# An attention and expert kernel: the router's early work in smaller steps, a pinned first phase, and products of zeros before the first tokens

## The chip, the cores and the metric

The kernel runs on one core of a Trainium2 chip. A core has a matrix engine (TensorE, PE in the profile, with its weight loads PEld), VectorE (DVE), ScalarE (ACT), GpSimd (POOL) and SyncE (SP), which issues transfers. Each engine takes its own list of instructions in order and waits on semaphores for the others. The metric is the time of one execution in microseconds (us), as the median of several runs; lower is better.

## The reference

```python
# attention: batch 8, heads 8, sequence 576, head size 64
scores = q @ k.T / 8 + slope[h] * -(i - j)      # kept where 0 <= i - j < 128
attn = softmax(scores); out = attn @ v
x = out.transpose(0, 2, 1, 3).reshape(4608, 512)
# experts: 8, each takes exactly 576 tokens
logits = x @ w_gate                              # 4608 x 8
# all 36864 (token, expert) pairs are gone through from the largest logit down;
# a token goes to the expert if it has none yet and the expert has room
for e in range(8):
    out[assigned == e] = relu(x[assigned == e] @ w1[e]) @ w2[e]   # 512 -> 1024 -> 512
```

## The kernel before

**Attention** goes over 32 pairs of heads (8 batches of 4 pairs). One iteration of its loop works on several pairs at once, in stages: `scores` and `least` of pair n (products of q and k on TensorE; then, on VectorE at L133, the bias and the row's least value), `exps` on ScalarE, `turn` and `turned` (u transposed on TensorE at L157, and copied to the tiles PT at L165, two of the four copies on VectorE), `av`, then `natural`, and `divide` (L240 to L255 on VectorE) of a pair four iterations older. Instructions put through `keep_in_program_order` stay in the order in which they are written; in attention that holds for TensorE, VectorE and ScalarE. The banks of PSUM that the transposes go to are four, and come free when the PT copies have been made.

**The router** needs, for each token, the best expert `am` and its logit `b` (`first_choice`: five operations b, ne, cand, am, OH). Logits `L_sb` have 36 columns of 128 tokens, four or five a batch; `logits` adds them up on GpSimd (L296 to L299) after a batch's last pair. Phase 0 finds the first expert that fills, by counting tokens over 64 thresholds in three rounds (`ends` for the range, `place`, `counts`, `enough`, `narrow`), then the list `idx` of its 576 tokens. Phases 1 to 7 do so for the others, in between the experts' products.

Some of phase 0 is done early. `early_counts` is a generator, made when the first 27 columns are there (batch 5), and `early_step` takes a step of it once a pair, directly behind `divide`. Its first step is `first_choice` over all 27 columns; then the range; then the indicators `ind` over 26 columns in two cuts, counted by 13 products of TensorE. In attention the router's instructions are pinned in written order through `OrderedCore`, so they show up in the trace under its line, L442, and `self.nc` is set back to the plain core before phase 0 itself, which is left to the scheduler.

**The experts** (`layer_moe`). `gather` issues five indirect transfers on GpSimd for an expert's tokens, `turn` transposes them (L832) and splits them into high and low parts (xh on ScalarE, xl on VectorE); weights come by SyncE as 512 KB chunks, and `split` makes their two parts. `layer1` (L853) and `layer2` (L878 to L881) are products in three terms. `slot` is called between pieces of these and hands out the router's steps, loads, splits and gathers. `layer2` goes over five pieces of tokens, t = 0 to 4; each result is stored by an indirect transfer of GpSimd (L891). Piece 4 has 64 tokens, and takes a copy and an addition on VectorE (L889, L890).

Of the kernel before, what the change touches and what calls it, by code (L numbers as in the profile page):

```python
# [25 lines left out]
def attention(tc, pools, qk_in, v_in, rel_in, C, x_dram, L_sb, router):  # L26
# [289 lines left out]
    for n in range(NPAIRS + LAG + 2):  # L316
# [92 lines left out]
WARM = 11  # L409
# [13 lines left out]
J = 64  # L423
CUTS = 2
STEPS = 3
FIRST = 27
EXACT_STEPS = 12
# [22 lines left out]
class Router:  # L450
# [5 lines left out]
    def __init__(self, tc, pools, C, L_sb):  # L456
# [3 lines left out]
        self.room, self.steps = None, iter(())  # L460
# [19 lines left out]
    def first_choice(self, L, b, am, OH, c0, c1):  # L480
# [8 lines left out]
        nc.vector.scalar_tensor_tensor(cand[:, :, 0:n], ne[:, :, 0:n], 16.0, eb, ALU.mult, ALU.add)  # L489
        nc.vector.tensor_reduce(am, cand[:, :, 0:n].rearrange("p e c -> p c e"), AX.X, ALU.min)  # L490
        nc.vector.tensor_tensor(OH, eb, bc(am.unsqueeze(1), [128, 8, n]), ALU.is_equal)

    def ends(self, b, top):
# [21 lines left out]
        if top:  # L515
# [6 lines left out]
            nc.vector.tensor_tensor(self.hi, ev[:, 1:2], sp, ALU.add)  # L522
        w = self.small("w")
# [23 lines left out]

    def counts(self, key, OH, th=None, c0=0, c1=NT):
# [6 lines left out]
        for a, z in zip(cuts, cuts[1:]):  # L555
            if th is None:
                nc.vector.tensor_tensor(ind[:, a:z, :].rearrange("p c (s o) -> p c s o", o=2),  # L557
                                        bc(key[:, a:z].unsqueeze(2), [128, z - a, J // 2, 2]),
                                        bc(self.C["i64"].rearrange("p (s o) -> p s o", o=2).unsqueeze(1), [128, z - a, J // 2, 2]),
                                        ALU.is_ge)  # L560
# [3 lines left out]
        yield WAITS[2]  # L564
        cnt = self.bank()
        for c in range(c0, c1, 2):
            nc.tensor.matmul(cnt[:, 0:16], ind[:, c:c + 2, :].rearrange("p c j -> p (c j)"),  # L567
                             OH[:, :, c:c + 2].rearrange("p e c -> p c e"), start=(c == c0), stop=(c == c1 - 2))
# [30 lines left out]

    def early_counts(self):  # L600
        nc = self.nc
        self.first_choice(self.L0, self.b0, self.am0, self.OH0, 0, FIRST)
        yield
        self.first = yield from self.ends(self.b0[:, 0:FIRST], True)
        lo, w, rw = self.first
        self.clamp(self.c0, self.b0, lo, w, 0, FIRST - 1)
        cnt = yield from self.counts(self.place(self.c0, lo, rw, 0, FIRST - 1), self.OH0, None, 0, FIRST - 1)
# [16 lines left out]
    def phase(self, k, exact=False):  # L624
# [6 lines left out]
        else:  # L631
            L, b, OH = self.L1, self.small("b", NT), rt.tile([128, 8, NT], BF, name="OH")
            am = rt.tile([128, NT], BF, name="am")
            self.first_choice(L, b, am, OH, 0, NT)
# [5 lines left out]
        else:  # L640
# [19 lines left out]
            nc.vector.scalar_tensor_tensor(self.hi, w, n[:, 0:1], low, ALU.mult, ALU.add)  # L660

        T1 = rt.tile([128, 8, NT], BF, name="T1")
        nc.vector.tensor_tensor(T1, OH, bc(sel.unsqueeze(1), [128, 8, NT]), ALU.mult)
        yield WAITS[4]
# [5 lines left out]
        keyv, mx, ef = self.small("keyv", 8), self.small("kmx"), self.small("ef")  # L670
        nc.vector.scalar_tensor_tensor(keyv, Dc, float(CAP), self.left, ALU.is_ge, ALU.mult)
        nc.vector.tensor_reduce(mx, keyv, AX.X, ALU.max)
        nc.vector.tensor_scalar(ef, mx, -1.0, 8.0, ALU.mult, ALU.add)

        m = rt.tile([128, NT], BF, name="m")
        nc.vector.scalar_tensor_tensor(m, am, ef[:, 0:1], sel, ALU.is_equal, ALU.mult)
# [4 lines left out]
        ei = rt.tile([128, 1], I32, name="ei", bufs=4)  # L681
        nc.vector.tensor_scalar(ei, ef, 7.0, None, ALU.min)
        self.ei[k] = ei
# [3 lines left out]
        nc.tensor.matmul(sp[:, 0:NT], self.C["tri"], m, start=False, stop=True)  # L687
        hi = self.small("hif", NT)
# [12 lines left out]
        if k == 0:  # L701
            nc.gpsimd.tensor_tensor(mv[:, :, 0, :], hOH, self.C["cc"], ALU.mult)
            nc.scalar.mul(mv[:, :, 1, :], hOH, self.C["pcol"][:, 0:1])
# [384 lines left out]
```

## Time and profile before

| | |
|---|---|
| median of 3 runs | 732.72 us (732.15 to 734.02) |
| the profiled execution | 731.64 us, its span 729.9 us |
| TensorE busy | 676.3 us (93%) |
| VectorE, ScalarE, GpSimd busy | 462.7, 330.8, 154.3 us |
| mean granted clock of TensorE | 0.964 |
| attention, to the last logits | 0 to 228 us |
| phase 0, to the first list of tokens | 228 to 247 us |
| first layer's first product to the last product | 258 to 716 us |

In the rows that follow, a timeline's row gives start, duration, engine, line, operation, output and inputs, shapes and count, and in brackets the engine's idle time ahead of it and what ended that. A window's row gives its length, then busy time and number of instructions for PE, PEld, DVE, ACT and POOL, then the granted clock (1.00 is full speed), the share of the transfer engines and GB/s.

### The profile page before, as it was taken

The numbers are of one execution on the slowest core, as the hardware profiler recorded it, in microseconds if no ns is written. First come the engines' busy times: TensorE is split into PE (matmuls) and PEld (weight loads), VectorE is DVE, ScalarE is ACT, GpSimd is POOL, SyncE is SP. The second block draws the span as 40 slices with busy tenths as digits, with TensorE's granted clock in tenths as the row PEclk, the third lists the DMA queues.
The fourth block names the chain that finished last, engine by engine and source line by source line (L and its number), as shares of the span: only waits on it lengthen the run. The fifth ranks groups of instructions, "written<-read, shape, count | busy, mean of one in ns | idle before, by whom it ended". The sixth has DMA issues, their size and how long they took to land.

```text
span 729.9 us, 19089 instructions
## 1 busy us (share of the span) xinstructions
PE 676.3 (93%) x7399; PEld 596.7 (82%) x7399; DVE 462.7 (63%) x1826; ACT 330.8 (45%) x990; POOL 154.3 (21%) x341
## 2 busy tenths in 40 slices
PE   7999999997976199999999999999999999999992
PEld 4998998996865188789889989989988988989981
DVE  6877777777775779869678828847856525413200
ACT  6988888887753252424232224324324324313100
POOL 4121222122120401423042131132123022011011
PEclk9999999999987589999999999999999999999996
DMA  8465655656312531617135235135135325101010
GB/s 298 137 219 165 211 187 167 203 169 201 97 54 67 194 103 58 253 52 242 69 118 200 84 106 173 59 116 159 59 118 170 102 92 184 60 30 37 1 44 26
DMA packets 35139, 92.73 MB, mean 127 GB/s; under 512 B 3808, under 2 KB 13152, under 8 KB 35040
## 3 DMA queue, kind: packets, MB, share of 16 engines
q1 hardware_dynamic: 29152, 72.55, 29.9%
q0 software_dynamic: 5888, 18.88, 8.0%
q8 instruction: 60, 0.98, 0.6%
q14 instruction: 39, 0.32, 0.2%
HBM read 72.54 MB, written 18.87 MB: 125 GB/s over the span
## 4 chain that ended last, share of the span: by engine, by line
PE 84%; DVE 8%; issue 2%; DMA 2%; POOL 1%; ACT 0%; POOLq 0%; SPq 0%; DVEq 0%
PE ph L853 27%; PE po L878 10%; PE po L879 10%; PE po L881 8%; PE s L53 7%; PE pt L53 6%; PE pt L157 6%; PE x L53 5%; DVE u L133 3%; PE pg L832 2%; PE m L567 2%; DMA g<-x,idx 2%; DMA rel_sb<-in_rel_dram 1%; DVE ind L557 1%; PE m L714 0%
## 5 line engine op out<-in xcount | busy, mean ns | idle before, releaser
L853 PE MATMUL ph<-xh,hl 128*128 128x288 f32 (+2 forms) x1024 | 192.6, 300 | 0.0
L853 PEld LDWEIGHTS ph<-xh,hl 128*128 128x128 f32 x1024 | 155.2, 189 | 0.9
L144 ACT ACTIVATE u<-u,mn 128x192 f32<-128x192 f32 (+2 forms) x288 | 123.8, 433 | 30.0 <-DVE mn L133 30.0
L878 PE MATMUL po<-hl,hh 128*128 128x512 f32 x320 | 129.3, 404 | 0.0
L879 PE MATMUL po<-hl,hh 128*128 128x512 f32 x320 | 125.0, 390 | 0.0
L853 PE MATMUL ph<-xl,hl 128*128 128x288 f32 (+2 forms) x512 | 116.1, 297 | 0.0
L859 ACT ACTIVATE hh<-ph 128x288 fp32r<-128x288 f32 (+2 forms) x128 | 46.6, 409 | 152.3 <-PE ph L853 143.6
L133 DVE CUSTOM_DVE_ANT_0 u<-s,bm 128x192 f32<-128x192 f32 x308 | 86.4, 333 | 41.6 <-PE s L53 41.1
L881 PE MATMUL po<-hl,hlo 128*128 128x512 f32 x256 | 100.4, 392 | 0.0
L806 DVE TENSOR_TENSOR hl<-raw,hl 128x512 fp32r<-128x512 f32 x128 | 84.8, 684 | 14.0 <-ACT hl L804 13.5
L891 POOL DMA_INDIRECT out_dram<-o,idx x40 | 44.1, 1102 | 205.6 <-ACT o L886 145.8
L853 PEld LDWEIGHTS ph<-xl,hl 128*128 128x128 f32 x512 | 84.2, 189 | 0.1
L834 DVE TENSOR_TENSOR xl<-pg,xh 128x512 fp32r<-128x512 f32 (+1 forms) x37 | 23.6, 639 | 86.6 <-ACT xh L833 86.6
L864 DVE SCALAR_TENSOR_TENSOR hlo<-ph,hh 128x288 fp32r<-128x288 f32 (+2 forms) x128 | 49.5, 417 | 40.8 <-ACT hh L859 40.3
L804 ACT CAST hl<-raw 128x1024 fp32r<-128x1024 f32 x64 | 65.4, 1048 | 17.1 <-DMA raw<-in_w_dram 9.3
L53 PE MATMUL s<-qk 64*64 64x192 f32 (+1 forms) x1112 | 70.5, 326 | 2.2 <-DVE mn L133 2.1
L878 PEld LDWEIGHTS po<-hl,hh 128*128 128x128 f32 x320 | 60.2, 188 | 11.5
L879 PEld LDWEIGHTS po<-hl,hh 128*128 128x128 f32 x320 | 60.2, 188 | 11.1
L157 PE MATMUL pt<-ident_sb,u 128*128 128x128 f32 x368 | 54.5, 283 | 9.8 <-DVE PT L165 8.3
L886 ACT COPY o<-po 128x512 f32<-128x512 f32 x32 | 18.8, 587 | 89.6 <-PE po L881 59.1
L881 PEld LDWEIGHTS po<-hl,hlo 128*128 128x128 f32 x256 | 48.0, 188 | 10.7
L815 POOL DMA_INDIRECT g<-x,idx x40 | 42.7, 1068 | 64.1 <-PE pg L832 34.3
(175 smaller groups left out, 928.4 us busy)
## 6 DMA issues: line engine op xcount, KB each, us to landing
raw<-in_w_dram SPq DMA_DIRECT2D x64, 512.0 KB, 4.5
qk<-in_qk_dram SPq DMA_DIRECT2D x32, 576.0 KB, 5.3
v<-in_v_dram SPq DMA_DIRECT2D x32, 288.0 KB, 4.0
x<-xb SPq DMA_DIRECT2D x14, 512.0 KB, 3.5
x<-xb SPq DMA_DIRECT2D x8, 128.0 KB, 2.2
x<-xb SPq DMA_DIRECT2D x4, 256.0 KB, 3.9
g<-x,idx POOLq DMA_INDIRECT x40
out_dram<-o,idx POOLq DMA_INDIRECT x40
```

The lines of the kernel that those rows point to most:

```text
L53: put(nc.tensor.matmul(out, w, a, start=start, stop=stop, skip_group_check=True))
L133: put(nc.vector.tensor_tensor_reduce(out=u[rows], in0=x[rows, c:c + 64 * m].rearrange("q (j k) -> q j k", k=64), in1=bm[n % NP][rows, y:y ...
L144: put(nc.scalar.activation(u, u, AF.Exp, bias=st["mn"][:, i:i + 1], scale=-1.0, accum_out=st["sm"][:, i:i + 1]))
L157: put(nc.tensor.transpose(ps[:, c:c + 128], u[:, o + 128 * j:o + 128 * j + 128], ident))
L804: self.last = nc.scalar.copy(hl[:, 0, :], raw)
L806: nc.vector.tensor_tensor(hl[:, 1, c:c + 512], raw[:, c:c + 512], hl[:, 0, c:c + 512].bitcast(F32), ALU.subtract)
L853: nc.tensor.matmul(pp[t], w[:, a, j, fo:fo + 128], x[:, j, cut[t]:cut[t + 1]], start=(j == 0 and a == 0 and x is xh), stop=(j == 3 and a = ...
L859: nc.scalar.activation(o, pp[t], AF.Relu)
L864: nc.vector.scalar_tensor_tensor(d, pp[t][:, c0:c1], 0.0, o[:, c0:c1].bitcast(F32), ALU.max, ALU.subtract)
L878: nc.tensor.matmul(po, a, wh, start=(f == 0), stop=False)
L879: nc.tensor.matmul(po, a, wl, start=False, stop=(f == 7 and t == 4))
L881: nc.tensor.matmul(po, hl[:, f, 128 * t:128 * t + 128], wh, start=False, stop=(f == 7))
```

## The change

Four things are altered.

- Early work. `first_choice` is cut into two steps (b, ne, cand; then am, OH) and made for each batch's own four or five columns. `self.steps` becomes a list of generators, and `early_step` takes one step a pair from the first of them, from batch 0 on and also where there is no transposing left. The range gets one step more, and the indicators come in three cuts over two steps. At the last batch whatever is left is run through. The codes of experts are reversed so that the choice is a maximum; this spares the operation `ef` ahead of `m`.
- Phase 0 is pinned in written order too (`r.nc = nc` now stands behind `r.start`). `hi`, `ef` and `ei` are written further down, and the first half of `mv` is made on VectorE in place of GpSimd.
- Products of zeros. `keep_warm` multiplies a tile of zeros: 10 products behind phase 0's last product, and 4 behind the transposes of each of the first two pieces of the first expert's tokens, all pinned, into a bank that nothing reads.
- The last expert's second layer goes over its pieces in the order 4, 0, 1, 2, 3, and the result of piece 3 is copied in halves by ScalarE and VectorE.

```diff
@@ attention, behind divide
-            if turns:
-                router.early_step(room)
+            router.early_step(room if turns else None)
@@ first_choice
-        nc.vector.scalar_tensor_tensor(cand[:, :, 0:n], ne[:, :, 0:n], 16.0, eb, ALU.mult, ALU.add)
-        nc.vector.tensor_reduce(am, cand[:, :, 0:n].rearrange("p e c -> p c e"), AX.X, ALU.min)
+        nc.vector.scalar_tensor_tensor(cand[:, :, 0:n], ne[:, :, 0:n], -16.0, eb, ALU.mult, ALU.add)
+        yield
+        nc.vector.tensor_reduce(am, cand[:, :, 0:n].rearrange("p e c -> p c e"), AX.X, ALU.max)
@@ ends, behind hi
+            yield 0
@@ early
-        if c1 == FIRST:
-            self.steps = self.early_counts()
-        elif c1 > FIRST:
-            self.first_choice(self.L0, self.b0, self.am0, self.OH0, c0, c1)
+        choice = self.first_choice(self.L0, self.b0, self.am0, self.OH0, c0, c1)
+        if c1 == NT:
+            for steps in self.steps + [choice]:
+                for _ in steps:
+                    pass
+            return
+        self.steps.append(choice)
+        if c1 == FIRST:
+            self.steps.append(self.early_counts())
@@ early_step
-        next(self.steps, None)
+        while self.steps:
+            try:
+                next(self.steps[0])
+                break
+            except StopIteration:
+                self.steps.pop(0)
@@ early_counts
-        self.first_choice(self.L0, self.b0, self.am0, self.OH0, 0, FIRST)
+        self.first = lo, w, rw = yield from self.ends(self.b0[:, 0:FIRST], True)
+        self.clamp(self.c0, self.b0, lo, w, 0, c1)
+        key = self.place(self.c0, lo, rw, 0, c1)
+        ind = rt.tile([128, NT, J], BF, name="ind", bufs=1)
         yield
...
+        for i in range(EARLY_CUTS):
+            a, z = (c1 * j // EARLY_CUTS for j in (i, i + 1))
+            self.indicate(ind, key, a, z)
+            if i % 2 == 1:
+                yield
+        cnt = self.count(ind, self.OH0, 0, c1)
@@ phase
-        nc.vector.tensor_scalar(ef, mx, -1.0, 8.0, ALU.mult, ALU.add)
...
-        nc.vector.scalar_tensor_tensor(m, am, ef[:, 0:1], sel, ALU.is_equal, ALU.mult)
+        nc.vector.scalar_tensor_tensor(m, am, mx[:, 0:1], sel, ALU.is_equal, ALU.mult)
...
-            nc.gpsimd.tensor_tensor(mv[:, :, 0, :], hOH, self.C["cc"], ALU.mult)
+            nc.vector.tensor_tensor(mv[:, :, 0, :], hOH, self.C["cc"], ALU.mult)
@@ MoE
+    def keep_warm(self, n):
+        for _ in range(n):
+            self.tc.keep_in_program_order(self.nc.tensor.matmul(self.idle, self.C["zero"][:, 0:128], self.C["zero"], start=True,
+                                                                stop=True))
...
+            if first and h < TURN0 - 1:
+                self.keep_warm(WARM1)
@@ layer2
-        for t in range(5):
+        for t in range(5) if not last else (4, 0, 1, 2, 3):
...
+            if last and t == 3:
+                nc.scalar.copy(o[:, 0:256], po[:, 0:256])
+                nc.vector.tensor_copy(o[:, 256:512], po[:, 256:512])
+            elif t < 4:
@@ layer_moe
+    with tc.issue_after(r.last_pe.ins):
+        m.idle = P["ps_h"].tile([128, 512], F32, name="ph")
+        m.keep_warm(WARM0)
@@ moe_attn_kernel
-            r.nc = nc
         P["ps_m"] = es.enter_context(tc.tile_pool(name="ps_m", bufs=1, space=PSUM))
         r.start(False)
+        r.nc = nc
```

What stands on VectorE at the end of batch 0 (the divide of its last pair, L240 to L255, then `least` of a younger pair, L133), before:

```order
L240 RECIPROCAL rs<-sd 128x10 [waits Pool_49]
L248 TENSOR_TENSOR Lp<-pt,rs 128x3x2x8 [waits DVE_49]
L255 TENSOR_TENSOR xb<-pt,rs 128x3x128
L248 TENSOR_TENSOR Lp<-pt,rs 128x2x2x8
L255 TENSOR_TENSOR xb<-pt,rs 128x2x128
L133 ISA u,mn<-s,bm_300 128x3x64 [waits PE_49]
```

and now:

```order
L240 RECIPROCAL rs<-sd 128x10 [waits Pool_49]
L248 TENSOR_TENSOR Lp<-pt,rs 128x3x2x8 [waits DVE_49]
L255 TENSOR_TENSOR xb<-pt,rs 128x3x128
L248 TENSOR_TENSOR Lp<-pt,rs 128x2x2x8
L255 TENSOR_TENSOR xb<-pt,rs 128x2x128
L442 TENSOR_REDUCE b_73<-L_sb 128x4 [waits Pool_49]
L442 TENSOR_TENSOR ne<-L_sb,b_73 128x8x4 [waits DVE_49]
L442 SCALAR_TENSOR_TENSOR cand<-ne,c_eb 128x8x4 [waits DVE_49]
L133 ISA u,mn<-s,bm_300 128x3x64 [waits PE_49]
```

Three operations on the batch's own logits, the first with a wait for GpSimd, have come between the divide and `least`; the same is found at the ends of batches 1 to 4. At batch 5 they take the place of five operations over 27 columns.

On GpSimd at the end of phase 0 (L731 and L734 make the next phase's logits from `pen`, L702 the first half of `mv`, L815 the gathers), before:

```order
L733 TENSOR_SCALAR Lt<-T_4719 128x288 [waits DVE_49]
L731 TENSOR_TENSOR L_4786<-L_sb,pen 128x288 [waits DVE_49]
L734 TENSOR_TENSOR L_72<-Lt,L_4786 128x288 [waits Pool_49]
L702 TENSOR_TENSOR mv<-hOH,c_cc 128x36x10 [waits DVE_49]
L815 DMA g<-x,idx 128x512 [waits DMAHW3_49,DMAHW2_49,DMAHW4_49,DMAHW1_49,DMAHW5_49,DMAHW0_49,DMAHW6_49,DVE_49,DMAHW7_49,PE_49,Activation_49]
L815 DMA g<-x,idx 128x512 x3
L815 DMA g<-x,idx 64x512
```

and now (L758, L756 and L759 are the former L733, L731 and L734, L840 the gathers):

```order
L758 TENSOR_SCALAR Lt<-T_4754 128x288 [waits DVE_49]
L840 DMA g<-x,idx 128x512 [waits DMAHW3_49,DMAHW2_49,DMAHW4_49,DMAHW1_49,DMAHW5_49,DMAHW0_49,DMAHW6_49,DVE_49,DMAHW7_49,PE_49,Activation_49]
L756 TENSOR_TENSOR L_4822<-L_sb,pen 128x288 [waits DVE_49]
L840 DMA g<-x,idx 128x512
L759 TENSOR_TENSOR L_72<-Lt,L_4822 128x288 [waits Pool_49]
L840 DMA g<-x,idx 128x512 x2
L840 DMA g<-x,idx 64x512
```

The two sums have moved from ahead of the gathers to between them, and `mv` is gone from this engine.

More of the change, by code (lines that the diff above doesn't have):

```diff
@@ L426 @@
 FIRST = 27
+EARLY_CUTS = 3
 EXACT_STEPS = 12
@@ L659, in phase @@
             nc.vector.tensor_scalar(sel, key[:, :, 0], 1.0, n[:, 0:1], ALU.add, ALU.is_ge)
-            nc.vector.scalar_tensor_tensor(self.hi, w, n[:, 0:1], low, ALU.mult, ALU.add)
         T1 = rt.tile([128, 8, NT], BF, name="T1")
         nc.vector.tensor_tensor(T1, OH, bc(sel.unsqueeze(1), [128, 8, NT]), ALU.mult)
+        if k < 7 and not exact:
+            nc.vector.scalar_tensor_tensor(self.hi, w, n[:, 0:1], low, ALU.mult, ALU.add)
         yield WAITS[4]
@@ L1000, in layer_moe @@
                 slot(k, i - 1)
-        for _ in m.layer2(W.pop((k, 1)), m.h, r.idx[k]):
+        for _ in m.layer2(W.pop((k, 1)), m.h, r.idx[k], k == E - 1):
             slot(k, i)
```

60 lines of the change are left out of this document (31 added, 29 removed).

## The prediction

> **What bounds the kernel now.** I read the page first, then TensorE's timeline up to 260 us for its idle times, then VectorE's timeline at those, then windows with the granted clock.
>
> ```profile
> PE 676.3 (93%) x7399; PEld 596.7 (82%) x7399; DVE 462.7 (63%) x1826; ACT 330.8 (45%) x990; POOL 154.3 (21%) x341
> ...
> 182.02 0.69 PE L157 MATMUL pt<-ident_sb,u 128*128 128x128 f32 x2 [3.67 <-DVE PT L165]
> 196.63 0.55 PE L157 MATMUL pt<-ident_sb,u 128*128 128x128 f32 x3 [0.40 <-DVE PT L165]
> 206.40 0.90 PE L157 MATMUL pt<-ident_sb,u 128*128 128x128 f32 x3 [3.37 <-DVE PT L165]
> 214.84 1.46 PE L53 MATMUL pt<-wn_sb,xT 128*128 128x144 f32 x10 [0.46 <-DVE part L442]
> 216.96 0.55 PE L157 MATMUL pt<-ident_sb,u 128*128 128x128 f32 x3 [0.65 <-DVE PT L165]
> ```
>
> TensorE is busy 93% of the span, so time is won or lost where it idles. Behind the first four pairs of attention it idles over 0.3 us only in these five places, and all lie at the router's early work. VectorE runs in written order there, with the early work ahead of `least` (L133) and of the PT copies that release TensorE:
>
> ```profile
> 160.26 0.36 DVE L133 CUSTOM_DVE_ANT_0 u<-s,bm 128x192 f32<-128x192 f32 x1 [1.23 <-PE s L53]
> ...
> 177.52 0.53 DVE L442 TENSOR_REDUCE b<-L_sb 128x27 f32<-128x216 f32 x1 [1.81 <-POOL L_sb L299]
> ...
> 179.66 0.29 DVE L133 CUSTOM_DVE_ANT_0 u<-s,bm 128x128 f32<-128x128 f32 x1
> ...
> 193.91 0.27 DVE L442 TENSOR_REDUCE em<-pt 2x1 f32<-2x128 f32 x1
> ...
> 194.41 0.34 DVE L133 CUSTOM_DVE_ANT_0 u<-s,bm 128x192 f32<-128x192 f32 x1
> ...
> 200.64 0.15 DVE L442 COPY ev<-pt 128x2 f32<-128x2 f32 x1
> ...
> 201.78 0.21 DVE L442 TENSOR_SCALAR w<-hi,lo 128x1 f32<-128x1 f32 x1
> ...
> 203.16 1.09 DVE L442 TENSOR_TENSOR ind<-kq,c_i 128x896 bf16<-128x896 bf16 x2
> 204.17 0.35 DVE L133 CUSTOM_DVE_ANT_0 u<-s,bm 128x192 f32<-128x192 f32 x1
> ...
> 213.14 0.21 DVE L442 TENSOR_REDUCE b<-L_sb 128x4 f32<-128x32 f32 x1 [1.52 <-POOL L_sb L298]
> ...
> 213.84 0.21 DVE L442 TENSOR_REDUCE am<-cand 128x4 bf16<-128x32 bf16 x1
> ...
> 214.33 0.16 DVE L442 COPY pt<-pt 64x8 f32<-64x8 f32 x1
> ```
>
> VectorE's delay passes to TensorE nearly whole. The step at 193.91 holds VectorE 0.50 us and TensorE then idles 0.40. The step from 200.64 to 204.17 holds it 3.53 and TensorE idles 3.37. At the end of batch 5 VectorE waits 1.81 for GpSimd's sums and works 2.14 (177.52 to 179.66), 3.95 in all, and TensorE idles 3.67. So 0.1 to 0.3 us is hidden, no more. VectorE's own idle of 1.23 (first row) is no cover: it lies behind the PT copies, where VectorE waits for scores.
>
> Long idles cost a second time. In windows of 3.41 us, with the clock in the column behind POOL:
>
> ```profile
> 11.21:14.63 3.42, 2.11 (x35) 1.38 (x33) 2.53 (x13) 3.42 (x16) 1.99 (x9) 1.00 1.02 411
> ...
> 178.47:181.88 3.41, 0.00 (x0) 0.00 (x0) 3.27 (x16) 1.89 (x9) 0.00 (x0) 1.00 0.81 268
> 181.88:185.29 3.41, 3.27 (x50) 2.94 (x54) 0.84 (x5) 0.84 (x3) 0.00 (x0) 0.50 0.00 0
> ...
> 202.36:205.77 3.41, 0.67 (x6) 0.45 (x4) 3.38 (x22) 1.21 (x5) 0.00 (x0) 1.00 0.00 0
> 205.77:209.19 3.42, 2.79 (x32) 1.92 (x33) 1.05 (x3) 1.52 (x7) 0.00 (x0) 0.50 0.02 5
> 209.19:212.60 3.41, 3.41 (x82) 3.30 (x83) 2.40 (x13) 2.09 (x9) 1.60 (x7) 0.50 0.01 2
> ...
> 226.25:229.67 3.42, 1.13 (x10) 0.92 (x8) 2.64 (x14) 3.42 (x19) 0.00 (x0) 1.00 0.27 79
> ...
> 256.97:260.39 3.42, 2.93 (x14) 2.59 (x15) 1.75 (x3) 1.60 (x3) 0.00 (x0) 0.50 0.19 55
> ```
>
> After windows with 0.00, 0.67 and 1.13 us of TensorE work the next runs at clock 0.50; after one with 2.11 it does not. Work done at 0.50 loses half its time: 1.64 of 3.27, and 3.10 of 2.79 + 3.41.
>
> **The change part by part.** The sum is made against the profiled execution, 731.64 us (span 729.9 and 1.74 around it); the median of the runs is 732.72.
>
> *New steps at the ends of batches 0 to 4.* The order puts `b`, `ne` and `cand` of each batch straight behind the divide of its last pair, with a wait for GpSimd, ahead of `least`. GpSimd's sums are unmoved, so the wait is what batches 5 and 6 show: 1.81 for odd batches, 1.52 for even ones. The three operations take 213.14 to 213.84, 0.70. That delays VectorE 2.5 or 2.2 us, behind which stand six `least`, both PT copies and then TensorE. With 0.3 and 0.1 hidden, TensorE idles 2.2 (batches 1, 3) or 2.1 (0, 2, 4). `am` and `OH` a pair later take 213.84 to 214.33, 0.49: idle 0.4 by the row at 196.63. Sum: 2 x 2.2 + 3 x 2.1 + 5 x 0.4 = **+12.7**. Lower bound 0 (all hidden), upper 15.
>
> *End of batch 5.* The idle of 3.67 becomes 2.2 and 0.4, and the half clock behind it (1.64) is dealt with below: **-2.7**.
>
> *Range and indicators.* 200.64 to 204.17 is cut into three places. `ev` to `hi` keeps 1.14 of VectorE (to 201.78), so 3.37 of idle becomes 1.0; and the 3.10 lost to the half clock goes: **-5.5**. `w` to `kq` (201.78 to 203.16, 1.4) takes the place of batch 6's work a pair later, where the idles 0.46 and 0.65 were: **+0.2**. The indicators, in three cuts (1.09), and batch 6's choice go to the last pairs, which have no `least`; TensorE's products cover them: 0, and 1.5 if that cover is gone.
>
> So without the clock attention takes 12.7 - 2.7 - 5.5 + 0.2 = +4.7 us.
>
> *The clock after the new stalls.* Six stalls of 2.1 to 2.2 us (batches 0 to 5) leave a window at least 1.2 us of work. Between 1.13 (clock falls) and 2.11 (it stays) no row decides. Taking the middle, 1.6 us of work or 1.8 of idle, a stall of 2.1 puts that much into one window from 1.9 of 3.4 us of start positions, a little over half; I take three of six. Each costs 1.64 where the rest is done in one window, 3.10 where it takes two; I take 2.0: **+6.0**. Bounds 0 and 6 x 3.1 = 18.6.
>
> *Phase 0 and the gathers.*
>
> ```profile
> 228.73 0.28 DVE L534 TENSOR_SCALAR c<-b,hi,low 128x10 f32<-128x10 f32 x1
> ...
> 229.65 0.20 DVE L442 TENSOR_TENSOR OH<-c_eb,am 128x40 bf16<-128x40 bf16 x1
> ...
> 239.90 0.15 DVE L672 TENSOR_REDUCE kmx<-keyv 128x1 f32<-128x8 f32 x1
> ...
> 240.62 0.24 DVE L676 SCALAR_TENSOR_TENSOR m<-am,ef,sel 128x36 bf16<-128x36 bf16 x1
> ...
> 241.48 0.22 DVE L678 TENSOR_TENSOR_SCAN run<-c_ones,m 128x36 bf16<-128x36 bf16 x1
> ...
> 291.60 0.34 DVE L705 TENSOR_TENSOR mv<-hOH,c_cc 128x360 bf16<-128x360 bf16 x1
> ...
> 240.01 0.67 POOL L731 TENSOR_TENSOR L<-L_sb,pen 128x288 f32<-128x288 f32 x1 [0.80 <-DVE ov L736]
> 240.75 0.79 POOL L734 TENSOR_TENSOR L<-Lt,L 128x288 f32<-128x288 f32 x1
> 243.41 1.51 POOL L702 TENSOR_TENSOR mv<-hOH,c_cc 128x360 bf16<-128x360 bf16 x1 [1.86 <-DVE hOH L694]
> ...
> 250.35 1.29 POOL L815 DMA_INDIRECT g<-x,idx  x1 [0.30 <-issue]
> ...
> 257.46 1.11 PE L832 MATMUL po<-ident_sb,g 128*128 128x128 f32 x4 [1.25 <-DMA g<-x,idx]
> ```
>
> In written order `c` starts behind `OH`, 0.95 later. `m` may start when `kmx` is done (240.05, not 240.62) and `run` when `m` is (240.86, not 241.48): -1.2. `mv` takes 0.34 on VectorE for 1.51 on GpSimd, but `loOH` waits for it: about -0.4. The indices come 0.65 earlier. But GpSimd's two sums (0.67, 0.79), which ran ahead of the gathers, now stand between the first, second and third gather, and TensorE's first layer waits for the third (257.46, 5.8 us after its issue ends at 251.64). It is issued 1.46 - 0.65 = 0.8 later, and `b` of phase 1 waits for the second sum on VectorE, with the split of later weights behind it; these have until the second chunk is due. Landing lies between -0.65 and +0.8: **0**.
>
> *Zeros.* The first layer starts at clock 0.50 and does 2.93 us of work there, half of it lost. Ten zeros before the first tokens take 3.7 us by this row, where eleven take 4.10:
>
> ```profile
> 1.22 4.10 PE L1022 MATMUL x<-zero 128*128 128x512 bf16 x11 [1.22 <-DVE pen L628]
> ```
>
> They fill a part of the wait for the first tokens; four more behind each of the first two turns (1.5 us each) keep TensorE busy from the first tokens on, so that a window full of work ends before the layer starts: **-1.4**, bounds -2.9 (clock up late in other executions) and +0.5 (zeros still running when the third tokens land).
>
> *End.*
>
> ```profile
> 715.82 0.69 DVE L889 COPY o<-po 64x512 f32<-64x512 f32 x1 [24.21 <-PE po L879]
> ...
> 717.56 0.90 POOL L891 DMA_INDIRECT out_dram<-o,idx  x1 [3.50 <-DVE o L890]
> ```
>
> The last store is issued 1.74 us after the copy starts. With halves on two engines (half of 0.69, then 0.28 as now from result to store) it is 0.65: -1.1. Twice the rows go out, which no row here prices apart: between 0 and 0.6, I take 0.3: **-0.8**.
>
> Sum: 4.7 + 6.0 + 0 - 1.4 - 0.8 = +8.5; 731.64 + 8.5 = **740.1 us**.
>
> **The rivals.**
>
> *No stall halves the clock.* 4.7 - 2.2 = +2.5, 734.1 us. For it: a window with 2.11 us of work kept its clock. Against: one with 1.13 did not, and mine may hold 1.2. It decides at the share of work below which the clock falls. The Trainium skill (TensorE: Matmul & The Clock Gate, Part 1: The HAM clock gate) says the clock halves after at least one idle window of a free-running 3413 ns; by that rule, taken strictly, no stall of 2.2 us could, and this rival would hold. The trace agrees on the window (all changes above are 3.41 us or multiples apart) but not on idleness: 0.67 and 1.13 us of work did not save the clock.
>
> *Every stall costs two windows.* 4.7 + 18.6 - 2.2 = +21, 752.7 us. For it: 205.77 to 212.60. Against: 181.88 to 185.29 needed one.
>
> *VectorE's idle hides the steps* (the other side). If the 1.23 us that VectorE waits for scores in each pair covered an early step, stalls of 2.2 would be 1.0, too short for the clock, and the 0.4 nothing: batches 0 to 4 +5.0, batch 5 -2.7 - 1.6, range step -3.4 - 3.1, pair after it -1.1: -6.9, with -2.2 elsewhere 722.5 us. For it: the many small idles of VectorE. Against: a step of 0.50 us already cost TensorE 0.40. It decides at a step shorter than 1.2 us.
>
> **How the numbers follow.** One to five stalls with a halved clock: 0.60, with 736 to 747 us as its own range. No stall: 0.20. Two windows each: 0.08. Hidden: 0.12. A measurement of this kernel tells 0.3%, 2.2 us, from no change: under 730.5 is faster, over 734.9 slower. The hidden case gives faster 0.12; no halved clock gives same 0.20; the rest, 0.68, is slower. The range 731 to 748 leaves out the hidden case and the two windows.
>
> **What would show it.** VectorE's `b` from `L_sb` seven times, five new ones near 49, 78, 105, 134 and 162 us (later where the clock fell), each idle 1.5 to 1.8 before it for GpSimd's `L_sb`; behind each, TensorE's transposes of `u` idle about 2 us for PT; clock 0.50 in the window after some of them. No idle over 2.5 us behind the range step; the first layer at clock 1.00; `m` within 0.3 us of `kmx`; the last store issued under 1 us after the last product. It is wrong if TensorE idles under 1 us at those batch ends, or if attention ends earlier than now.

## The result, and the profile after

The changed kernel takes **740.51 us** (median of 4, 739.65 to 742.02) against 732.43 us before (731.91 to 734.02; one run more than in the table above): a ratio of 1.0109, 95% interval 1.0086 to 1.0132. It is slower by about 8 us. The profiled execution took 739.65 us, with a span of 737.8 us, against 731.64 and 729.9.

The page has TensorE's line, and the group of the transposes of u, whose idle time shows what grew (before: 9.8 us of idle, 8.3 of them for PT).

```profile
PE 682.8 (93%) x7416; PEld 599.2 (81%) x7417; DVE 468.0 (63%) x1854; ACT 331.4 (45%) x990; POOL 154.5 (21%) x340
...
L157 PE MATMUL pt<-ident_sb,u 128*128 128x128 f32 x368 | 54.2, 282 | 17.0 <-DVE PT L165 15.6
```

Two timelines of the changed kernel, VectorE's `b` and range rows first, then TensorE's idle times over 0.3 us up to the end of attention (the brackets hold the idle time in front of an instruction and what ended it):

```profile
49.40 0.21 DVE L442 TENSOR_REDUCE b<-L_sb 128x4 f32<-128x32 f32 x1 [1.54 <-POOL L_sb L298]
...
78.82 0.22 DVE L442 TENSOR_REDUCE b<-L_sb 128x5 f32<-128x40 f32 x1 [1.82 <-POOL L_sb L299]
...
213.78 0.15 DVE L442 COPY ev<-pt 128x2 f32<-128x2 f32 x1
...
237.36 0.22 DVE L442 TENSOR_REDUCE b<-L_sb 128x5 f32<-128x40 f32 x1
```

```profile
52.21 0.55 PE L157 MATMUL pt<-ident_sb,u 128*128 128x128 f32 x3 [1.95 <-DVE PT L165]
81.79 0.44 PE L157 MATMUL pt<-ident_sb,u 128*128 128x128 f32 x2 [2.14 <-DVE PT L165]
...
195.31 0.44 PE L157 MATMUL pt<-ident_sb,u 128*128 128x128 f32 x2 [2.14 <-DVE PT L165]
209.76 0.44 PE L157 MATMUL pt<-ident_sb,u 128*128 128x128 f32 x2 [0.40 <-DVE PT L165]
217.02 0.55 PE L157 MATMUL pt<-ident_sb,u 128*128 128x128 f32 x3 [0.86 <-DVE PT L165]
224.80 0.44 PE L157 MATMUL pt<-ident_sb,u 128*128 128x128 f32 x2 [1.30 <-DVE PT L165]
```

The five new steps stand where they were forecast, with waits of 1.54 and 1.82 us for GpSimd's sums. Behind each TensorE idles 1.95 or 2.14 us; the other ends, at 109.53, 138.11 and 166.75, have the same two numbers. The range step's idle fell from 3.37 to 0.86.

Divided at three moments (VectorE's last `b`, the first layer's first product, the end of the last product), the two spans compare so:

| stage | before | after | difference |
|---|---|---|---|
| start to the last `b` | 228.35 | 237.36 | +9.0 |
| last `b` to the first layer's first product | 29.87 | 29.31 | -0.56 |
| first product to the end of the last | 457.56 | 457.07 | -0.49 |
| end of the last product to the end of the span | 14.09 | 14.05 | -0.04 |

All of the loss lies in attention, and what was meant for the stages behind it brought 1.1 us.

The clock: windows of 3.41 us of the changed kernel, laid on the moments at which the clock changes (columns: busy us and instructions of PE, PEld, DVE, ACT, POOL, then the granted clock).

```profile
50.05:53.46 3.41, 1.46 (x27) 1.08 (x29) 2.52 (x15) 2.53 (x11) 0.00 (x0) 1.00 0.95 304
53.46:56.87 3.41, 3.41 (x86) 3.33 (x80) 2.71 (x15) 2.50 (x11) 0.95 (x5) 0.50 0.07 24
...
77.35:80.77 3.42, 2.25 (x17) 1.82 (x15) 1.87 (x13) 1.52 (x7) 1.44 (x5) 1.00 0.83 258
80.77:84.18 3.41, 2.39 (x80) 2.23 (x84) 2.02 (x9) 1.95 (x8) 0.00 (x0) 1.00 0.54 198
...
135.38:138.79 3.41, 1.23 (x17) 0.81 (x18) 3.04 (x16) 2.19 (x10) 0.03 (x1) 1.00 0.82 253
...
193.41:196.82 3.41, 1.51 (x38) 1.34 (x42) 2.27 (x12) 2.54 (x11) 0.00 (x0) 1.00 0.73 255
196.82:200.23 3.41, 3.41 (x88) 3.33 (x80) 2.92 (x17) 2.62 (x11) 1.11 (x6) 0.50 0.03 7
```

Three of the six stalls halved the clock, for one window each: those that left 1.46, 1.23 and 1.51 us of work in a window. A stall of the same 2.14 us that fell across two windows, with 2.25 and 2.39 us of work left, did not. This is one execution; the windows of the others are not on record.

### The profile page after: what moved, and what is told of

It is laid out like the page before. It is cut to its first block, busy times and chain, and to the rows that moved or that the text cites. A ratio compares the mean times of both kernels' runs of the same rounds, so it can differ in the third digit from the quotient of the medians.

```text
span 737.8 us, 19156 instructions
## 1 busy us (share of the span) xinstructions
PE 682.8 (93%) x7416; PEld 599.2 (81%) x7417; DVE 468.0 (63%) x1854; ACT 331.4 (45%) x990; POOL 154.5 (21%) x340
## 4 chain that ended last, share of the span: by engine, by line
PE 78%; DVE 13%; DMA 3%; POOL 2%; issue 2%; ACT 1%; SPq 0%; POOLq 0%; DVEq 0%; ACTq 0%
PE ph L887 25%; PE po L912 10%; PE po L913 10%; PE po L915 8%; PE s L53 6%; PE pt L53 5%; PE pt L157 4%; DVE u L133 4%; PE x L53 4%; PE pg L864 2%; PE m L575 1%; DMA craw<-in_cst_dram 1%; DVE PT L165 1%; DMA g<-x,idx 1%; DMA qk<-in_qk_dram 1%
## 5 line engine op out<-in xcount | busy, mean ns | idle before, releaser
L133 DVE CUSTOM_DVE_ANT_0 u<-s,bm 128x192 f32<-128x192 f32 x308 | 86.4, 333 | 41.2 <-PE s L53 40.7
L157 PEld LDWEIGHTS pt<-ident_sb,u 128*128 128x128 f32 x368 | 39.1, 140 | 27.7 <-DVE PT L165 18.4
L840 POOL DMA_INDIRECT g<-x,idx x40 | 42.9, 1073 | 68.7 <-PE pg L864 33.8
```

Of the source, the lines that this page charges most:

```text
L133: put(nc.vector.tensor_tensor_reduce(out=u[rows], in0=x[rows, c:c + 64 * m].rearrange("q (j k) -> q j k", k=64), in1=bm[n % NP][rows, y:y ...
L157: put(nc.tensor.transpose(ps[:, c:c + 128], u[:, o + 128 * j:o + 128 * j + 128], ident))
```

## The experiments

"Attention" below is the time from GpSimd's sums of batch 0 (48.84 us before, 49.12 in the changed kernel) to VectorE's last `b`, which leaves out how an execution begins: 179.5 us before, 188.2 after the change. The kernels ran in three groups, each with the kernel before measured again beside it: 732.50 us for the first four below, 731.53 for the one without zeros and the three of the section behind it, 733.17 for the other three. Ratios are to these, so between groups they compare better than times.

### The wait alone, put into the kernel before

```diff
     def early(self, c0, c1):
+        if c1 < FIRST:
+            self.nc.vector.tensor_reduce(self.b0[:, c0:c1], self.L0[:, :, c0:c1].rearrange("p e c -> p c e"), AX.X, ALU.max)
```

> The kernel before, with one operation added at each of the ends of batches 0 to 4: the reduction b from L_sb over the four or five columns just made, ahead of least, with its wait for GpSimd's sums. Its results are written again later by the choice over 27 columns, so nothing else changes. It prices the wait alone. Theory (the wait delays TensorE nearly whole): five times 1.5 to 1.8 of wait and 0.2 of operation, less 0.1 to 0.3 hidden: +7.5 to +9, and up to 2 us more where a stall of 1.6 us halves the clock: 740 to 743 us. Rival (the wait is covered by TensorE's queue, and the operations of the whole step make the cost): 732 to 734 us.

Measured: 742.89 us, ratio 1.0137 (1.0107 to 1.0167). Its timelines (VectorE, then TensorE):

```profile
52.92 0.21 DVE L442 TENSOR_REDUCE b<-L_sb 128x4 f32<-128x32 f32 x1 [1.52 <-POOL L_sb L298]
```

```profile
55.26 0.55 PE L157 MATMUL pt<-ident_sb,u 128*128 128x128 f32 x3 [1.49 <-DVE PT L165]
83.01 0.44 PE L157 MATMUL pt<-ident_sb,u 128*128 128x128 f32 x2 [1.66 <-DVE PT L165]
```

Attention takes 188.4 us, 8.9 more than before, 7.8 of it the five idle times (3 of 1.49, 2 of 1.66). None of the five halved the clock; the windows with the least work had 1.75 us of it. So the wait with one operation of 0.2 us is most of what the five steps cost. (In the profiled execution, of 744.98 us, the clock was also halved from 12.95 to 23.2 us, ahead of the first batch's end; GpSimd's sums of batch 0 came 3.8 us later than before, which "attention" leaves out.)

### The wait away, all operations kept

```diff
         self.steps.append(choice)
+        self.fresh = c1 < FIRST
...
     def early_step(self, room):
+        if getattr(self, "fresh", False):
+            self.fresh = False
+            return
```

> The changed kernel, with one thing altered: at the ends of batches 0 to 4 the first early step (b, ne, cand) is taken one pair of heads later than now, when GpSimd has long made the sums; every instruction stays. Theory (the wait of VectorE for GpSimd's sums, 1.5 to 1.8 us, is what makes the stalls of the changed kernel): the waits ahead of b from L_sb of batches 0 to 4 are gone, TensorE's idle behind these steps falls from 1.95 to 2.14 us to about 0.6, none of the five halves the clock, and the time falls by 5 x 1.5 and the 1 to 2 us of clock that batches 0 and 3 cost: 730 to 732 us. Rival A (the extra operations themselves cost, the wait is covered by something else): 738 to 741 us. Rival B (the time of attention is set by TensorE's own work and the later steps only move the idle to another place): idle over 1 us somewhere else in the same pairs, 738 us or more.

Measured: 729.14 us, ratio 0.9948 (0.993 to 0.9965), 11.4 us under the changed kernel, a little under the forecast, and faster than the kernel before. VectorE's and TensorE's rows at the end of batch 0:

```profile
54.46 0.20 DVE L442 TENSOR_REDUCE b<-L_sb 128x4 f32<-128x32 f32 x1
```

```profile
57.38 0.55 PE L157 MATMUL pt<-ident_sb,u 128*128 128x128 f32 x3 [0.50 <-DVE PT L165]
```

The wait is gone, the idle is 0.50 to 0.52 at each of the five, and the clock is never halved in attention. Attention takes 177.25 us, 11.0 less: five waits (3 x 1.54 + 2 x 1.82 = 8.3) and the halved clocks with what followed from them. Only the moment of the steps was altered, so the rival that the added operations were the cost falls. They do cost what is left: 3.6 us against the 173.7 of the next kernel, which does without them.

### One choice over 27 columns, as before; the rest of the change kept

```diff
-        choice = self.first_choice(self.L0, self.b0, self.am0, self.OH0, c0, c1)
+        if c1 < FIRST:
+            return
+        choice = self.first_choice(self.L0, self.b0, self.am0, self.OH0, 0 if c1 == FIRST else c0, c1)
```

> The changed kernel without separate choices at the ends of batches 0 to 4: one choice over the 27 columns at the end of batch 5, in two steps with its wait for GpSimd as in the kernel before; the cut-up range step, the indicators in three pieces, the pinned phase 0, the zeros and the end stay. Theory (the five new stalls cost 14.5 us against the pairs of the kernel before, the rest of the change wins about 7): five stalls gone, and the stall at the end of batch 5 grows by about 1.5 to 3 us and may halve the clock: 726 to 729 us. Rival (the new steps cost nothing much, and what is slower lies behind attention, in phase 0, the zeros or the end): 736 to 741 us.

Measured: 725.67 us, ratio 0.9912 (0.9884 to 0.994). This is just under the forecast. Attention 173.7 us: the five early ends cost the changed kernel 14.6 us. The one long stall left did not halve the clock, as this kernel's TensorE row and the window that it lies in show:

```profile
180.83 0.44 PE L157 MATMUL pt<-ident_sb,u 128*128 128x128 f32 x2 [2.80 <-DVE PT L165]
```

```profile
176.26:179.68 3.42, 1.73 (x13) 1.30 (x10) 2.41 (x12) 1.03 (x6) 0.98 (x4) 1.00 1.03 316
```

### The steps in VectorE's idle time

The step of a pair is moved from behind `divide` to behind the two PT copies of the next iteration.

```diff
             room = ps[3][:, 384:512]
+        if ends:
+            router.early_step(room if turns else bank)
...
-            router.early_step(room if turns else None)
...
```

> The changed kernel with the early step of each pair moved: it no longer stands behind the divide, ahead of least and the PT copies, but a pair later and behind the two PT copies, where VectorE waits 1.2 us for the scores. Same instructions. Theory (a step costs TensorE what it holds VectorE ahead of the PT copies, and in VectorE's idle behind them it costs nothing): TensorE idles under 0.5 us at all batch ends and behind the range step, no halved clock in attention: 740.5 - 14.5 (five ends) - about 2 (batch 5 and the range step) = 721 to 725 us. Rival A (the idle of 1.2 us is no cover, since least of the next scores comes late by as much as the step takes and the turns of u with it): stalls of 0.4 to 0.7 us stay at each step, 728 to 732 us. Rival B (the steps do not matter): 738 to 741 us.

Measured: 721.46 us, ratio 0.9853 (0.9825 to 0.988). Attention 170.2 us, 7.0 less than with the wait away alone. TensorE's only idle times over 0.3 us in attention behind the first pairs are two of 1.60 us:

```profile
191.24 0.27 PE L443 MATMUL pt<-ident_sb,ext 128*2 128x128 f32 x1 [1.60 <-DVE PT L165]
...
199.22 0.38 PE L443 MATMUL pt<-ed,craw 2*128 2x2 f32 x2 [1.60 <-DVE PT L165]
```

None of the six ends has such an idle time. VectorE's 1.2 us behind the PT copies do hide a step of 0.7 us, and one of 1.1. Rival A, idle of 0.4 to 0.7 at each step, falls.

### The place alone, for the long steps of the kernel before

```diff
             room = ps[3][:, 384:512]
+        if ends and turns:
+            router.early_step(room)
...
-            if turns:
-                router.early_step(room)
```

> The kernel before, with its early steps (27 columns chosen at once, range, indicators) put behind the two PT copies instead of behind the divide; its steps are not cut up. It separates the place from the cutting. Theory (idle of 1.2 us hides a step up to its length): the wait of 1.81 us is gone, of the 2.14 us of choice about 0.9 is left, of the range step's 3.5 us about 2.3; the two halved clocks gone or cheaper: 732.5 - 3 - 1 - 2 to 4 = 724 to 727 us. Rival (only cutting up helps, the place does nothing for long steps): 730 to 733 us.

Measured: 731.19 us, ratio 0.997 (0.9956 to 0.9983). The rival held: the place alone brings about 2 us (1.2 to 3.2 by the interval; 0.7 of it shows in attention, 178.8 us against 179.5). The idle times only move. The choice over 27 columns costs TensorE an idle of 0.58 instead of 3.67, but the small products of the range step and the 13 of the indicators now stand in TensorE's queue where they wait for VectorE:

```profile
192.31 0.27 PE L442 MATMUL pt<-ident_sb,ext 128*2 128x128 f32 x1 [1.60 <-DVE PT L165]
200.28 0.38 PE L442 MATMUL pt<-ed,craw 2*128 2x2 f32 x2 [1.59 <-DVE PT L165]
212.80 0.55 PE L442 MATMUL pt<-OH,ind 128*128 128x16 bf16 x13 [4.24 <-DVE PT L165]
```

The clock was halved twice in attention, as before. So cutting up in the old place loses 8 us, the new place without cutting wins about 2, and both together win 11.

### The small products behind the ten of `natural`

In the kernel with the steps in VectorE's idle, the call is moved a few lines down, behind `natural`.

```diff
-        if ends:
-            router.early_step(room if turns else bank)
...
             natural(k - 2, N)
+            router.early_step(room if turns else bank)
```

> The kernel with the early steps in VectorE's idle (721.5 us), each step now written behind the ten products that give the natural layout, not ahead of them. VectorE's order is the same; on TensorE the range step's small products no longer stand in front of those ten, where two of them waited 1.60 us each for the PT copies. Theory (those two waits are all that the early work still costs attention): both idles gone, 721.5 - 3.2 = about 718.3 us. Rival (TensorE waits as long for something else in these two pairs, scores or PT): 720.5 to 721.5 us.

Measured: 721.04 us, ratio 0.9824 (0.9792 to 0.9855). The idle times of 1.60 became 0.37:

```profile
191.09 0.27 PE L442 MATMUL pt<-ident_sb,ext 128*2 128x128 f32 x1 [0.37 <-DVE PT L165]
197.84 0.38 PE L442 MATMUL pt<-ed,craw 2*128 2x2 f32 x2 [0.37 <-DVE PT L165]
```

Attention takes 168.4 us, 1.8 less, but the profiled execution has lost it again by the first layer, which begins 248.18 us into the span, where it began at 248.22. "The leanest form" below tells why. By the time the rival held; by the ratios the gain is 2.1 us, within the intervals of the two.

### Without products of zeros

```diff
-    with tc.issue_after(r.last_pe.ins):
-        m.idle = P["ps_h"].tile([128, 512], F32, name="ph")
-        m.keep_warm(WARM0)
...
-            if first and h < TURN0 - 1:
-                self.keep_warm(WARM1)
```

> The kernel with the early steps in VectorE's idle (721.5 us) without any products of zeros between the router and the first layer. Theory (zeros are worth 1.4 us): the first layer starts at the halved clock and loses about half of 2 to 3 us of work: 722.5 to 723.5 us. Rival (the zeros only take the place of waits and put off the turns by as much as they win; the clock falls again between the ten and the first tokens anyway): 721 to 722 us, with the first layer's first product 1 to 2 us earlier behind the indices and at the halved clock for a window.

Measured: 721.80 us, ratio 0.9871 (0.9845 to 0.9896), no difference from 721.46 that the intervals could tell. The rows are the rival's. First the changed kernel's zeros on TensorE, then the turns without zeros:

```profile
254.60 3.92 PE L848 MATMUL ph<-zero 128*128 128x512 bf16 x9 [0.22 <-issue]
262.09 1.11 PE L864 MATMUL pg<-ident_sb,g 128*128 128x128 f32 x4 [3.57 <-DMA g<-x,idx]
263.00 1.91 PE L848 MATMUL ph<-zero 128*128 128x512 bf16 x4
```

```profile
244.00 1.11 PE L865 MATMUL pg<-ident_sb,g 128*128 128x128 f32 x4 [7.36 <-DMA g<-x,idx]
246.27 1.11 PE L865 MATMUL po<-ident_sb,g 128*128 128x128 f32 x4 [1.15 <-DMA g<-x,idx]
...
248.10 1.20 PE L886 MATMUL ph<-xh,hl 128*128 128x256 f32 x4
```

The zeros ahead of the tokens brought the clock up at 258.3 us, but TensorE then waited 3.57 us for the first tokens and the clock fell again at 261.7. So the first turn ran at half clock after all, and the four zeros behind it took 1.91 us at that clock in front of the second turn. Without zeros the first layer begins 28.5 us behind the last `b` instead of 28.9 (0.4 earlier, not 1 to 2), at half clock for 1.3 us; from the last `b` to the end of the last product the two profiled executions take 485.3 and 485.6 us.

### The end, phase 0, and GpSimd's sums

Three more of the same kernel. The first takes the last expert's pieces in the old order, each copied in one piece (`layer2(..., last=False)`).

> The kernel with the early steps in VectorE's idle (721.5 us), and the last expert's second layer in the order of the kernel before: 64 odd tokens last, each block copied in one piece. Prediction's term: the new end wins 0.8 us, so 722.3 us. Rival (the new end wins nothing: its halves are copied one behind the other, 0.37 and 0.42 us, and the last store has 128 rows for 64): 721.3 to 721.8 us, the last store issued 1.7 us behind the last product instead of 1.1, and the span ending 12.3 us behind that issue instead of 12.9.

Measured: 722.94 us, ratio 0.9882 (0.9854 to 0.9911), above both forecasts, with runs from 720.63 to 727.04, so the time does not tell; in the profiled execution 2.1 us were lost ahead of batch 0's sums, where the clock was halved from 13.28 to 20.10. The stage itself tells: the last product's end to the end of the span is 14.25 us against 14.20. As the rival has it, the new end is worth nothing, under 0.1 us. The changed kernel's own rows say why:

```profile
723.82 0.37 ACT L920 COPY o<-po 128x256 f32<-128x256 f32 x1 [4.89 <-PE po L915]
```

```profile
724.23 0.42 DVE L921 COPY o<-po 128x256 f32<-128x256 f32 x1 [20.80 <-ACT o L920]
```

```profile
724.93 0.97 POOL L928 DMA_INDIRECT out_dram<-o,idx  x1 [4.75 <-DVE o L921]
```

The halves go to one tile, and VectorE's half waited for ScalarE's. The last store is issued 1.11 us behind the start of the first half's copy (before: 1.74 behind the start of the copy), and the span ends 12.86 us behind the issue of those 128 rows (before, 64 rows: 12.31). So 0.6 us is won ahead of the issue and as much lost behind it.

The second leaves phase 0 to the scheduler, with mv on GpSimd.

```diff
+        r.nc = nc
         r.start(False)
-        r.nc = nc
...
-            nc.vector.tensor_tensor(mv[:, :, 0, :], hOH, self.C["cc"], ALU.mult)
+            self.tc.nc.gpsimd.tensor_tensor(mv[:, :, 0, :], hOH, self.C["cc"], ALU.mult)
```

> The kernel with the early steps in VectorE's idle (721.5 us), and phase 0 left to the scheduler again, with mv on GpSimd as in the kernel before. Prediction's term for the pinned order and mv is 0 at the first layer (indices 0.65 us earlier, gathers that GpSimd's sums delay by 0.8): 721.5 us, the indices 18.2 us behind the last b instead of 17.8, the sums ahead of the gathers. Rival A (the indices decide): 722.0 to 722.3 us. Rival B (the sums between the gathers decide): 720.5 us.

Measured: 721.33 us, ratio 0.9857 (0.983 to 0.9884): no difference, as the prediction's 0 has it. Its profiled execution does begin the first layer 29.75 us behind the last `b`, 0.85 later than with the pinned order; the medians cannot show so little.

The third writes `pen`, `left` and GpSimd's three operations ahead of `hi`, so that GpSimd is done before the gathers.

```diff
+        if k < 7:
+            self.pen = self.small("pen", 8)
+            ...
         hi = self.small("hif", NT)
```

> The kernel with the early steps in VectorE's idle (721.5 us), and in it the two operations pen and left and GpSimd's three operations on L (which now run between the first three gathers, 0.90 and 0.80 us) written ahead of hi, so that GpSimd has done the sums before the indices come. Theory A (the first layer waits for the third token block, so its lateness counts): the third gather is issued 3.8 us behind the indices instead of 5.5, the first layer begins about 1.5 us earlier: 719.5 to 720.5 us. Theory B (the zeros behind the turns, 1.9 us at the halved clock, or the weights set the beginning instead): gathers earlier by the same, the layer at most 0.5 us earlier: 721 to 722 us.

Measured: 723.56 us, ratio 0.989 (0.9865 to 0.9915), above both forecasts, though the intervals of the two overlap; the first layer began 29.7 us behind the last `b`, not 1.5 us earlier than 28.9 but later. GpSimd's two sums and the issue of its third gather, and VectorE beside the sums:

```profile
233.21 0.67 POOL L719 TENSOR_TENSOR L<-L_sb,pen 128x288 f32<-128x288 f32 x1 [2.15 <-DVE pen L443]
233.96 0.88 POOL L722 TENSOR_TENSOR L<-Lt,L 128x288 f32<-128x288 f32 x1
...
241.87 2.57 POOL L841 DMA_INDIRECT g<-x,idx  x1 [0.30 <-issue]
```

```profile
233.39 0.53 DVE L443 TENSOR_SCALAR hif<-hif 128x36 f32<-128x36 f32 x1
...
234.22 0.82 DVE L443 TENSOR_TENSOR hOH<-c_h,hv 128x360 bf16<-128x360 bf16 x1
```

With the sums elsewhere the same two take 0.18 and 0.35 us. They end at 233.92 and 235.04, within 0.2 us behind the sums (233.88 and 234.84). VectorE lost 0.8 us beside them ahead of the indices, so the third gather was begun at 241.87, only 0.7 earlier than 242.56. Issuing it then took GpSimd 2.57 us, where it took 0.96, so it was out 0.9 later, and its tokens were turned at 248.63 instead of 247.76, 0.9 later too. VectorE worked on parts of the weights (`hl`) from 241.74 to 243.63; whether that held the issue up is not shown. Nothing was won by having the sums done first; what a third gather 1.5 us earlier would bring stays open.

### The leanest form

Steps behind `natural`, no zeros, odd tokens first at the end but the last result copied in one piece by ScalarE. The first two are the edits shown above; the third is:

```diff
-            if last and t == 3:
-                nc.scalar.copy(o[:, 0:256], po[:, 0:256])
-                nc.vector.tensor_copy(o[:, 256:512], po[:, 256:512])
-            elif t < 4:
+            if t < 4:
```

> As the one with the steps behind the ten products, without any products of zeros, and with the last result copied in one piece by ScalarE (odd tokens still first). Theory (zeros are worth nothing; two halves one behind the other, 0.37 and 0.42 us, are 0.2 us longer than one copy of 0.59): 0 to 0.3 us under the one with zeros and halves, 718 to 718.5 us. Rival (zeros are worth 1.4 us): 719.5 us or more.

Measured: **719.40 us**, ratio 0.9806 (0.9777 to 0.9835), faster than both kernels, and between the theory and the rival. Attention 168.4 us; the first layer begins 28.4 us behind the last `b`, against 30.8 with zeros, where the four zeros ran at half clock behind both the first and the second turn:

```profile
242.26 1.11 PE L864 MATMUL pg<-ident_sb,g 128*128 128x128 f32 x4 [3.97 <-DMA g<-x,idx]
243.16 1.91 PE L848 MATMUL ph<-zero 128*128 128x512 bf16 x4
245.72 1.91 PE L848 MATMUL ph<-zero 128*128 128x512 bf16 x4
```

The layers take 458.0 us against 456.7, so 1.3 of those 2.4 us come back in the first layer at half clock. The last store is issued 0.86 us behind the start of its copy, where the two halves took 1.11. From the last `b` to the end of the last product the profiled execution without zeros takes 486.4 us, with them 487.5. The medians with and without zeros differ by 1.6 us here and by 0.3 the other way in the pair above, both less than the intervals are wide. So in neither pair of profiled executions do the zeros win anything; what they are worth in the median, to within 1.4 us, is not shown.

## Why the prediction was right, and where its sizes were off

The forecast of 740.1 us was right: 740.51. The mechanism was the forecast one, shown from both sides: the wait put in alone costs 8.9 us of attention, and taken away gives 11.0. That the sum came so near is luck in part: the profiled executions differ by 7.9 us in span where +8.5 was forecast, because a loss taken 3.4 us too large (the clock) stands against gains taken 1.1 too large (zeros, end and phase 0 together) and a loss of 1.2 us put at nothing (the last pairs).

**New steps of batches 0 to 4 (+12.7)**: right. Where the clock did not fall, the two pairs behind an end are 2.7 us (batch 1) and 2.5 us (batches 2 and 4) longer than in the kernel before, by the starts of `divide`; over five ends that is 13.0. The idle of 1.95 and 2.14 us was forecast as 2.1 and 2.2, that of `am` and `OH` as 0.4 and measured as 0.26.

**The clock after the stalls (+6.0)**: three of six, as taken, but 2.0 us each was mis-sized. Batch 0, whose stall halved the clock, is 1.0 us longer than batch 2; batch 3 is 0.9 longer than batch 1; batch 5, set against the kernel with the wait away, where the same idle of 2.14 us did not halve the clock, is 0.7 longer (16.60 us for its two pairs against 15.90). Three are 2.6. The step that failed is "work done at 0.50 loses half its time". The row of 80.77 shows a window behind a stall at full clock: it holds 2.39 us of work, with VectorE's own delays between. At half clock TensorE is busy all of 3.41 us and does what takes 1.71, so 0.7 is lost by this estimate: the slower clock fills gaps that are there anyway. The border, taken as 1.6 us of work in the middle between 1.13 and 2.11, nearly held behind the first pairs of attention: windows with 1.23, 1.37, 1.46, 1.51 and 1.63 us of work were followed by half clock, those with 1.73 (row above), 1.75 and 1.81 were not. One window, in the kernel with the place alone, breaks it:

```profile
197.14:200.55 3.41, 1.82 (x21) 1.48 (x13) 3.04 (x17) 3.34 (x15) 0.80 (x4) 1.00 0.26 87
200.55:203.97 3.42, 3.42 (x19) 3.06 (x18) 3.03 (x19) 0.14 (x2) 0.00 (x0) 0.50 0.00 0
```

0.27 of its 1.82 us are the two products of 2x2 elements at 200.28. Whether such small products count as work for the clock is not shown.

**Range and indicators (-5.5), end of batch 5 (-2.7), the step w to kq (+0.2)**: the pairs at the end of batch 5 gained 1.7 with one halved clock in them, so 2.4 without. From the start of `divide` of pair 25 to that of pair 28 (counted from 0) 24.75 us became 19.47, a gain of 5.3 as forecast: the idle of 3.37 is 0.86, and the two windows at half clock are gone. But from pair 28 to the last `b` 10.95 us became 12.11, where the forecast had 0 because "TensorE's products cover them". The indicators' 13 products, which stood at 208.92 before, now stand among the last pairs' products on TensorE, with an idle time for VectorE, and those go on at 230.82:

```profile
229.83 0.41 PE L442 MATMUL pt<-OH,ind 128*128 128x16 bf16 x8
230.57 0.32 PE L442 MATMUL pt<-OH,ind 128*128 128x16 bf16 x5 [0.32 <-DVE ind L442]
```

The forecast's own 1.5 for a cover that is gone was nearer than its 0. In all attention lost 8.7 us (9.0 with the start of the execution), not 10.7. The terms add up to 9.1; one pair of the kernel before, at the end of batch 3, took 0.35 us longer than in the kernel with the wait alone.

**Phase 0 and the gathers (0)**: last `b` to the indices went from 18.21 to 17.81, where -0.65 was forecast. The written order cost 1.0 us up to `kmx`, as forecast, and the part from `ex` to the indices gained 0.3 instead of 0.4. That `m` and `run` would start 1.2 us earlier is right (1.1 from `kmx` to `ex`), but the reason given, the scheduler's order, was not the whole. VectorE's rows of the kernel before, which stand beside GpSimd's sums of 240.01 and 240.75:

```profile
240.16 0.54 DVE L729 SCALAR_TENSOR_TENSOR left<-keyv,kmx,left 128x8 f32<-128x8 f32 x1
...
240.85 0.71 DVE L738 SCALAR_TENSOR_TENSOR ov<-kmx,ov 128x1 f32<-128x1 f32 x1
```

`left` takes 0.22 and `ov` 0.16 in the changed kernel, where no sum runs beside them, and here they end at 240.70 and 241.56, when the sums end (240.68 and 241.54). So the sums seem to have held VectorE up; the pinned order moved them away and in among the gathers.

**Zeros (-1.4) and the end (-0.8)**: both wrong. The first layer does begin at full clock, as forecast (at 266.67, the clock up at 265.09). But the clock that came up for the ten zeros fell again in the 3.57 us before the first tokens, which the forecast left out, and the zeros behind the turns then ran at half clock and put off the next turn. The halves of the last result were taken to run side by side, and went one behind the other, so the last store was issued 1.19 us behind the last product, not under 1; the 128 rows cost 0.55 us behind the issue, where 0.3 was taken. Of the 2.2 us that both terms held, the three stages behind attention gained 1.1 in all, phase 0's 0.4 among them; the layers' 0.49 is within what they differ from kernel to kernel (456.0 to 458.3 us).

**The rivals.** "No stall halves the clock" (734.1) fell: three did. The Trainium skill (TensorE: Matmul & The Clock Gate, Part 1: The HAM clock gate) has the clock fall after at least one idle window; if idle means without work, the rows with 1.23 to 1.51 us of work in the window disagree. "Two windows each" fell: each took one. "VectorE's idle hides the steps" fell for the order as written, since the idle lies behind what the steps delay; 722.5 us was its price, and 721.46 was measured once the steps were moved there.

## What to carry to other kernels

A step that is cut smaller pays its own wait and its own hand-over each time: before cutting, look at what its first instruction waits for and at what is queued behind it, and take the step when its input has long been there. An idle time of an engine is cover only for work that is written inside it, and the small products that such a step issues on another engine need their own place in that engine's queue. Price a halved clock by the work that the window behind a stall holds at full clock, not by its length: here that was 0.7 to 1.0 us a window, not half of 3.41.

## What the runs showed of the hardware that was not expected

Some VectorE operations take longer beside a sum of 128x288 numbers on GpSimd, as if they waited for its end: four that take 0.16 to 0.35 us by themselves took 0.53 to 0.82, and each ended within 0.2 us behind the sum beside it (240.70 and 240.68, 241.56 and 241.54, 233.92 and 233.88, 235.04 and 234.84). The Trainium skill (SBUF — State Buffer, Who interferes with whom) has such a pair block, not share, where a VectorE operation has two inputs in SBUF and GpSimd's reads SBUF; three of the four rows agree, and the fourth, `hif`, is a tensor_scalar with one tensor as input, for which the same section names another mode that takes the shared port.

A stall of 2.80 us kept the clock and, in the changed kernel, one of 1.95 lost it while two others of 1.95 kept it: where the stall lies against the windows decides more than its length. At the start of the execution the border does not hold: there a window with 2.06 us of work was followed by half clock in two kernels (the wait alone, the old end), and windows with 2.05 in others were not. These two executions reached batch 0's sums 2 to 4 us later than the others (51.19 and 52.64 us, elsewhere 48.79 to 49.53), which is as much as several of the terms above.
